# A new order of loads, stores and pieces in a cross-covariance attention kernel with a mixture of adapters

## The chip, the cores and the metric

The kernel runs on 1 core of one Trainium2 chip. The metric is device time in microseconds (us), the median of three runs.

## The reference

There are four batches, and in each of them q, k and v are 6400 x 256 in fp32. An attention over channels comes first, then a layer that adds two of eight small adapters to each row.

```python
qn = q / (np.linalg.norm(q, axis=1, keepdims=True) + 1e-06)
kn = k / (np.linalg.norm(k, axis=1, keepdims=True) + 1e-06)
s = kn.transpose(0, 2, 1) @ qn / tau          # 256 x 256 for each batch
a = np.exp(s - s.max(-1, keepdims=True)); a /= a.sum(-1, keepdims=True) + 1e-09
x = (v @ a).reshape(25600, 256)
logits = x @ w_gate                           # 8 experts, the best 2 are kept
w = softmax(logits of these two)
out = x + sum over the two experts of w * (x @ A[e]) @ B[e]      # A[e] is 256 x 16
```

Every input is read once and the output is written once: 78.91 MB read and 26.21 MB written by the profile's account.

## The kernel before, in words

**Tiling.** A batch of 6400 rows lies on 128 partitions as 50 columns of 256 numbers. One column of one input is 128 KB in HBM. q and k come in two loads of 25 columns each (`QK`, L248), some of them cut further (`PARTS`, L464). v comes in pieces of 10 columns, five for each batch, and `V` (L249) says which loads bring one piece and which bring two. The loads of q, k and v are issued by GpSimd (POOL, L690) and turn fp32 into bf16 on the way; only the first five columns of q and k come without it, from two other queues (L687). The stores are issued by SyncE (SP, L1033).

**What is done with the data.** For each column `do_G` (L699) adds k^T q to an accumulator in PSUM (L705), and on request k^T k and q^T q, whose diagonals are the squared norms (L709, L713). For a group of five columns named in `OFF` (L467) the squares are made elsewhere: ScalarE squares (L726) and VectorE adds (L732). When the 50 columns of a batch are in, a short chain (norms, L771, exp, L818, transposes, `waA`, `a`) makes the matrix a and the products of a with the gate and with A. From then on each piece of v can be worked on: ten transposes (`T`, L890) and their copies (`Te`), then logits and adapter inputs. Where the piece is in `MERGED` (L475) one matmul over 136 columns gives both (`ZL`, L914) and four copies bring them to SBUF; otherwise 8 columns of logits come first (`log`, L928, one copy) and the 128 of the adapter inputs later (`Z`, L981), read straight from PSUM. Eight small VectorE and ScalarE steps make the gate weights, `Ze` (L992) multiplies, `gzT` (L1004) transposes, `Y` (L1017 and L1022) makes the output in five parts, `Ye` (L872 or L874) copies them into a y slot, and the store leaves from there.

**What sets the order.** Nothing is scheduled by hand, line by line. `make_plan` (L281) lists every step with a duration, dependencies and a rank; `Plan.run` (L108) goes through them with a model of the engines, the clock and the DMA, and the order that comes out is what is emitted for each engine. The constants before the kernel's function steer this:

- `WORDS` (L454): the order of the loads. `q10` stands for the loads of q and k of batch 1, half 0, and `v32` for the load number 2 of v of batch 3.
- `STORE` (L255): buffers. There are 4 slots for halves of q and k, 4 slots for pieces of v, 4 for transposed pieces (`vT`) and 7 for pieces of the output (`y`). A load waits for its slots, and two pieces in one load need two neighbouring slots. At most 8 loads are outstanding (L79).
- `PAIRS` (L251): pieces whose output goes out in one store of 20 columns. `FINE` (L465): pieces of the last batch that go out in several stores.
- `HOLD` (L460): a store with an entry waits for the landing of the load that the entry names. This keeps the DMA engines for loads first and keeps stores in hand for later. The y slots stay taken as long. An entry for the second piece of a pair has no effect.
- `AHEAD` (L458) moves `T` and `ZL` forward in rank; `SQ` (L473) moves the squares; `WARM` (L457) allows for matmuls that only keep TensorE's clock up.

Of the kernel before, what the change touches and what calls it, by code (L numbers as in the profile page):

```python
# [71 lines left out]
class Plan:  # L72
# [35 lines left out]
    def run(self, head):  # L108
# [137 lines left out]
UNITS = ((0, 4), (4, 4), (8, 2))  # L246
GATE = {"eq1": "ga", "t": "ga", "th": "ga", "g2": "ga", "lm": "gb", "mask": "gb"}
QK = ((0, 25), (25, 25))  # L248
V = (((0, 1), (1, 1), (2, 2), (4, 1)), ((0, 1), (1, 1), (2, 1), (3, 2)), ((0, 1), (1, 1), (2, 1), (3, 1),  # L249
        (4, 1)), ((0, 1), (1, 1), (2, 2), (4, 1)))  # L250
PAIRS = {(0, 1), (1, 0), (2, 0), (2, 3)}  # L251

GROUPS = ((0, 5), (5, 5), (10, 5), (15, 5), (20, 5), (25, 5), (30, 5), (35, 5), (40, 5), (45, 5))
ZUNITS = ((0, 3), (3, 3), (6, 2), (8, 2))
# [3 lines left out]
def group_of(c):  # L258
    return max(g for g, (c0, _) in enumerate(GROUPS) if c0 <= c)
# [6 lines left out]
def load_of(b, i):  # L266
    return max(g for g, (i0, _) in enumerate(V[b]) if i0 <= i)


def pieces(b, i):  # L270

    return next((((b, j), (b, j + 1)) for j in (i - 1, i) if (b, j) in PAIRS), ((b, i),))


def held_by(p, b, i):

    kind, d, j = HOLD[b, i]
    return [k for k in p.steps if k[:4] == ("load", kind, d, load_of(d, j) if kind == "v" else j)][-1]


def make_plan(B, order, ahead):  # L281
# [6 lines left out]
    for kind, b, i in order:  # L288
        if kind == "v":
            c0, n = V[b][i]  # L290
            p.add(("load", "v", b, i, c0 * PC, n * PC), {}, (), 0, take=(("v", tuple((b, c0 + j) for j in range(n))),),
                  size=COL * n * PC)
            continue
        for c, n in PARTS.get((b, i), QK[i:i + 1]):
            for h in "qk":
# [3 lines left out]
    for h in "qk":  # L299
        p.add(("cast", h), {"ACT": 1.2}, [("load", h, 0, 0) + PARTS[0, 0][0]], 0)  # L300
    for b in range(B):

        for i, (c0, n) in enumerate(QK):
            for c in range(c0, c0 + n):
                deps = [k for k in p.steps if k[0] == "load" and k[2:4] == (b, i) and k[1] != "v"
                        and k[4] <= c < k[4] + k[5]]
                if (b, c) < (0, PARTS[0, 0][0][1]):
                    deps = [("cast", k[1]) for k in deps]
                if c:
                    deps.append(("G", b, c - 1))  # L310
                elif b:
                    deps += [(x, b - 1, ic) for x in ("n2", "accs") for ic in range(2)]
                p.add(("G", b, c), {"PE": 0.445 - 0.1135 * sum((b, group_of(c), w) in OFF for w in "kq")}, deps,
                      pos["qk", b, i] if b else -50,
# [3 lines left out]
        for w in "kq":  # L318
            halves = [x for x in range(len(GROUPS)) if (b, x, w) in OFF]
            if halves:  # L320
# [3 lines left out]
            for x, g in enumerate(halves):  # L324
# [3 lines left out]
                      [k for k in p.steps if k[:4] == ("load", w, b, i) and k[4] < c + n and c < k[4] + k[5]]  # L328
                      + [("cast", w)] * ((b, c) == (0, 0)), pos["qk", b, i] - SQ, take=(("ssq", ((w, b),)) if x == 0 else ("sq", ((w, b, g),)),),
                      give=(("qk", (w, b, i)),))  # L330
                if x:
                    p.add(("add", w, b, g), {"DVE": 0.069 + 0.2668 * n},
                          [("sq", w, b, g), before], pos["qk", b, i] - SQ, give=(("sq", (w, b, g)),))
                    before = ("add", w, b, g)
# [6 lines left out]
        if b == 0:  # L341
            p.add(("wts",), {"DVE": 2.12}, [("load", "k", 0, len(QK) - 1) + PARTS[0, len(QK) - 1][1]], -200)

# [21 lines left out]
        for i in range(NP):  # L365
            v = load_of(b, i)
            c0, n0 = V[b][v]
            x = pos["v", b, v] + 0.3 * (i - c0)
            for u, (c, n) in enumerate(UNITS):
# [4 lines left out]
                      [("T", b, i, u)], x - ahead, give=(("bank", ("T", b, i, u)),))  # L374
            merged = (b, i) in MERGED
            if merged:
# [54 lines left out]
    for b in range(B):  # L431
        for i in range(NP):
            x = pos["v", b, load_of(b, i)]
            names = pieces(b, i)
            if (b, i) != names[0]:
                continue
            parts = FINE[i] if b == B - 1 and i in FINE else ((0, PC * len(names)),)
            for c, n in parts:
                p.add(("store", b, i, c, n), {"SP": 0.46},
                      [("Ye", b, i + c0 // PC, c0 % PC) for c0 in range(c, c + n, 2)]  # L440
                      + ([held_by(p, b, i)] if (b, i) in HOLD else []), x, size=COL * n,
                      give=tuple(("y", x) for x in names) if c + n == PC * len(names) else ())
# [3 lines left out]
def make_order(words):  # L446

    order = [("qk", 0, i) for i in range(len(QK))]
    for w in words.split():
# [1 line left out]
    return order  # L451


WORDS = ('q10 v00 q11 v01 v02 q20 v03 v10 q21 v11 v12 v13 q30 v20 v21 v22 v23 q31 v24 v30 v31 v32 v33')  # L454
HEAD = 5.05
COL = 1.024 * 1.17647 / 32
WARM = 150  # L457
AHEAD = 5.7  # L458

HOLD = {(0, 0): ('v', 3, 2), (0, 1): ('v', 1, 4), (0, 2): ('v', 1, 2), (0, 3): ('k', 3, 1), (1, 0): ('v', 2,  # L460
        4), (1, 1): ('k', 3, 2), (1, 2): ('k', 3, 1), (1, 3): ('v', 3, 1), (2, 0): ('v', 3, 3), (2, 1):
        ('k', 2, 0), (2, 2): ('v', 1, 3), (2, 3): ('v', 2, 2), (3, 3): ('v', 2, 2)}

PARTS = {(0, 0): ((0, 5), (5, 12), (17, 8)), (0, 1): ((25, 17), (42, 8)), (3, 1): ((25, 17), (42, 8))}  # L464
FINE = {3: ((0, 6), (6, 4)), 4: ((0, 4), (4, 4), (8, 2))}  # L465
SPLIT, SHARES = set(), ()
OFF = {(0, 0, 'k'), (0, 0, 'q'), (0, 1, 'k'), (0, 2, 'k'), (0, 2, 'q'), (0, 3, 'k'), (0, 4, 'k'), (0, 4,  # L467
        'q'), (0, 5, 'q'), (0, 6, 'k'), (0, 7, 'k'), (0, 9, 'q'), (1, 0, 'k'), (1, 2, 'k'), (1, 3, 'k'), (1,
        3, 'q'), (1, 6, 'k'), (1, 6, 'q'), (1, 7, 'q'), (1, 8, 'k'), (1, 9, 'k'), (2, 0, 'k'), (2, 1, 'k'),
        (2, 3, 'k'), (2, 3, 'q'), (2, 4, 'k'), (2, 5, 'k'), (2, 5, 'q'), (2, 6, 'k'), (2, 6, 'q'), (2, 7,  # L470
        'q'), (2, 8, 'q'), (2, 9, 'q'), (3, 0, 'k'), (3, 1, 'k'), (3, 2, 'k'), (3, 2, 'q'), (3, 3, 'q'), (3,
        5, 'k'), (3, 5, 'q'), (3, 7, 'q'), (3, 8, 'q'), (3, 9, 'q')}
SQ = 0  # L473
SAFE = 1.3
MERGED = {(0, 0), (0, 1), (0, 2), (0, 3), (0, 4), (1, 0), (1, 1), (1, 2), (1, 3), (1, 4), (2, 0), (2, 2),  # L475
        (2, 3), (2, 4), (3, 0), (3, 1), (3, 2), (3, 3), (3, 4)}


def first_ahead(nc, names):
# [90 lines left out]
def kernel(  # L570
# [72 lines left out]
    scrap = const.tile([1, 16], BF16, name="scrap")  # L643
    order = make_order(WORDS)
    plan = make_plan(B, order, AHEAD)
    steps = plan.run(HEAD)
# [52 lines left out]
    def do_G(s, b, c):  # L699
# [4 lines left out]
        for ic in range(CC):  # L704
            nc.tensor.matmul(  # L705
                acc[ic][:, 0:256], kt[:, j, ic::CC], qt[:, j, :],
                start=c == 0, stop=False, skip_group_check=True)
            if (b, group_of(c), "k") not in OFF:
                nc.tensor.matmul(  # L709
                    acc[ic][:, 256:384], kt[:, j, ic::CC], kt[:, j, ic::CC],  # L710
                    start=False, stop=False, skip_group_check=True)
        for ic in range(0 if (b, group_of(c), "q") in OFF else CC):
            nc.tensor.matmul(  # L713
# [42 lines left out]
    def do_n2(s, b, ic):  # L756
# [5 lines left out]
        for x, w in enumerate("kq"):  # L762
            if all((b, g, w) in OFF for g in range(len(GROUPS))):
                continue
# [6 lines left out]
    def do_rsqrt(s, b):  # L771
        n2 = st[b]["n2"]
        for x, w in enumerate("kq"):
            part = held.get(("bank", ("n2p", w, b)))
            if part is None:
                continue
            if all((b, g, w) in OFF for g in range(len(GROUPS))):
                nc.vector.tensor_copy(n2[:, x, :], part)
# [97 lines left out]
    def do_cast(s, what):  # L876
        nc.scalar.copy(held["qk", (what, 0, 0), ""][:, 0:PARTS[0, 0][0][1], :], W[what])  # L877

# [58 lines left out]
    def gate_step(name):  # L937
        def f(s, b, i):
            if (b, i) in MERGED and name == "m1":
                gate_tiles(s, b, i)  # L940
# [87 lines left out]
    def do_store(s, b, i, c, n):  # L1028
# [3 lines left out]
        for rows in SHARES if (b, i) in SPLIT else (P,):  # L1032
            r = nc.sync.dma_start(out_v[b, p:p + rows, lo:lo + n, :], Y[p:p + rows, at_y:at_y + n, :])  # L1033
            if (b, i) in HOLD and not p:
                tc.add_manual_dep(r.ins, loaded[held_by(plan, b, i)],
# [62 lines left out]
```

## Time and profile before

| | |
|---|---|
| runs | 251.01, 251.12, 251.16 us, median 251.12 |
| profiled execution: span, first to last instruction | 246.2 us |
| last packet of a store in the profiled execution, from the first instruction on | 249.6 us |
| last store issued, and its landing | 244.8 us, 5.1 us later |
| TensorE, VectorE, ScalarE busy | 218.3, 184.8, 169.7 us |
| packet time on the 16 DMA engines, all queues | 102.3% of the span |

The time of the profiled execution as a whole isn't given apart from its span; the runs are 4.9 us longer than the span, and stores still move in 3.4 us of that. A share over 100% for the DMA engines means that records of neighbouring packets on an engine overlap in time. A load takes eight packets on each of the 16 engines (one for each partition row) and one of 4 bytes that reports its landing; a store likewise.

### The profile page before, as it was taken

How to read it: one execution, taken by the hardware profiler on the slowest of the kernel's cores; microseconds unless marked ns; L12 is line 12 of the kernel's file. 1: busy time of each engine (PE TensorE's matmuls, PEld its weight loads, DVE VectorE, ACT ScalarE, POOL GpSimd, SP SyncE). 2: the span in 40 equal slices, each digit the busy share in tenths (PEclk: the TensorE clock that was granted, in tenths of full speed). 3: DMA queues.
4: the chain of work that ended last, by engine and by line, in shares of the span. 5: the costliest groups of instructions: out<-in, count | busy, mean ns of one | idle time of the engine just before them, and what ended most of it. 6: DMA issues, size and time to landing. Idle time of an engine off the chain costs nothing.

```text
span 246.2 us, 5334 instructions
## 1 busy us (share of the span) xinstructions
PE 218.3 (89%) x2208; PEld 179.7 (73%) x2025; DVE 184.8 (75%) x511; ACT 169.7 (69%) x316; POOL 21.8 (9%) x45
## 2 busy tenths in 40 slices
PE   0687298498999999999969999999999999999996
PEld 0255175176877998978959788899776799999985
DVE  0045578558869689999974898998989578788681
ACT  2944442275666769888776787999453599988885
POOL 7000202100030011000201003110000000000000
PEclk9999769679999999999997999999999999999999
DMA  8999999999999999999999999999999999999999
GB/s 275 215 216 216 208 221 227 201 225 219 206 220 224 209 210 231 208 224 201 260 281 268 316 276 207 216 217 223 308 216 303 380 373 282 323 407 433 419 429 409
DMA packets 8788, 65.85 MB, mean 268 GB/s; under 512 B 994, under 2 KB 1378, under 8 KB 4796
## 3 DMA queue, kind: packets, MB, share of 16 engines
q0 software_dynamic: 5616, 38.67, 75.4%
q1 hardware_dynamic: 2812, 26.06, 25.6%
q10 hardware_dynamic: 336, 0.79, 0.8%
q8 instruction: 16, 0.26, 0.4%
q14 instruction: 8, 0.07, 0.1%
HBM read 78.91 MB, written 26.21 MB: 427 GB/s over the span
## 4 chain that ended last, share of the span: by engine, by line
DMA 39%; PE 37%; issue 11%; DVE 9%; ACT 3%; POOL 1%; POOLq 0%; ACTq 0%
DMA v<-in_v_dram 27%; PE Y_ps L1017 10%; DMA qk<-in_q_dram 6%; PE acc L705 6%; PE Y_ps L1022 5%; PE ZL_ps L914 5%; DMA qk<-in_k_dram 5%; PE T_ps L890 5%; PE gzT_ps L1004 3%; DVE gz L992 3%; DVE ssq L732 2%; PE acc L709 2%; ACT y L872 1%; DVE y L874 1%; PE acc L713 1%
## 5 line engine op out<-in xcount | busy, mean ns | idle before, releaser
L705 PE MATMUL acc<-qk 128*128 128x256 bf16 x400 | 77.6, 288 | 15.3 <-ACT qk L877 8.3
L732 DVE TENSOR_TENSOR ssq<-ssq,sq 128x1280 f32<-128x1280 f32 x35 | 52.0, 1487 | 21.9 <-ACT sq L726 21.9
L705 PEld LDWEIGHTS <-qk 128*128 128x128 bf16 x400 | 39.7, 104 | 31.0 <-DMA qk<-in_k_dram 9.8
L872 ACT COPY y<-Y_ps 128x512 f32<-128x512 f32 x87 | 50.8, 594 | 15.2 <-PE Y_ps L1022 12.9
L726 ACT ACTIVATE sq<-qk 128x1280 f32<-128x1280 bf16 x35 | 44.8, 1279 | 23.5 <-DVE ssq L732 20.7
L1017 PE MATMUL Y_ps<-a_bf,vT 128*128 128x256 bf16 x400 | 60.0, 272 | 0.1
L1017 PEld LDWEIGHTS <-vT 128*128 128x128 bf16 x400 | 38.3, 98 | 5.1 <-issue 0.4
L1022 PE MATMUL Y_ps<-ball,gzT 128*128 128x256 bf16 x200 | 38.2, 273 | 0.0
L992 DVE TENSOR_TENSOR gz<-zl,gatega 128x256 bf16<-128x256 f32 x95 | 35.4, 444 | 0.5
L709 PE MATMUL acc<-qk 128*128 128x128 bf16 x170 | 32.7, 225 | 0.0
L890 PE MATMUL T_ps<-ident,v 128*128 128x128 f32 x200 | 27.2, 284 | 3.9 <-DMA v<-in_v_dram 3.6
L713 PE MATMUL acc<-qk 128*128 128x128 bf16 x200 | 28.7, 227 | 0.0
L872 ACT COPY vT<-T_ps 128x512 f32<-128x512 f32 (+1 forms) x47 | 23.0, 545 | 5.5 <-PE T_ps L890 5.4
L890 PEld LDWEIGHTS T_ps<-ident,v 128*128 128x128 f32 x200 | 22.9, 146 | 5.3 <-issue 3.3
L914 PE MATMUL ZL_ps<-waA_sb,vT 128*128 128x136 bf16 x380 | 26.3, 223 | 0.4 <-ACT y L872 0.3
L914 PEld LDWEIGHTS <-vT 128*128 128x128 bf16 x380 | 23.8, 98 | 1.4 <-issue 0.4
L713 PEld LDWEIGHTS <-qk 128*128 128x128 bf16 x200 | 19.1, 102 | 5.0
L872 ACT COPY zl<-ZL_ps 128x408 f32<-128x408 f32 (+1 forms) x50 | 19.9, 457 | 3.4 <-PE ZL_ps L914 3.4
L1004 PE MATMUL gzT_ps<-ident,gz 128*128 128x128 f32 x100 | 19.8, 281 | 1.8 <-DVE gz L992 1.5
L1022 PEld LDWEIGHTS <-gzT 128*128 128x128 bf16 x200 | 19.5, 98 | 2.3
L874 DVE COPY zl<-ZL_ps 128x272 f32<-128x272 f32 (+1 forms) x26 | 12.7, 498 | 6.8 <-PE ZL_ps L914 6.6
L690 POOL DMA_DIRECT2D qk<-in_q_dram x11 | 6.1, 552 | 111.8 <-ACT y L872 41.2
(78 smaller groups left out, 217.2 us busy)
## 6 DMA issues: line engine op xcount, KB each, us to landing
out_dram<-y SPq DMA_DIRECT2D x10, 1280.0 KB, 11.8
out_dram<-y SPq DMA_DIRECT2D x4, 2560.0 KB, 17.5
v<-in_v_dram POOLq DMA_DIRECT2D x14, 640.0 KB, 28.0
qk<-in_q_dram POOLq DMA_DIRECT2D x5, 1600.0 KB, 15.9
qk<-in_k_dram POOLq DMA_DIRECT2D x5, 1600.0 KB, 23.0
v<-in_v_dram POOLq DMA_DIRECT2D x3, 1280.0 KB, 28.5
qk<-in_q_dram POOLq DMA_DIRECT2D x2, 1088.0 KB, 19.5
qk<-in_k_dram POOLq DMA_DIRECT2D x2, 1088.0 KB, 25.0
```

The lines of the kernel that those rows point to most:

```text
L705: nc.tensor.matmul(acc[ic][:, 0:256], kt[:, j, ic::CC], qt[:, j, :], start=c == 0, stop=False, skip_group_check=True)
L709: nc.tensor.matmul(acc[ic][:, 256:384], kt[:, j, ic::CC], kt[:, j, ic::CC], start=False, stop=False, skip_group_check=True)
L713: nc.tensor.matmul(acc[ic][:, 384:512], qt[:, j, ic * P:(ic + 1) * P], qt[:, j, ic * P:(ic + 1) * P], start=False, stop=c == NC - 1, skip_ ...
L726: nc.scalar.activation(out[:, 0:n, :], t[:, j:j + n, :], ACT.Square)
L732: nc.vector.tensor_tensor(out=t, in0=t, in1=held["sq", (w, b, g), ""][:, 0:n, :], op=OP.add)
L872: nc.scalar.copy(out, in_)
L890: nc.tensor.matmul(ps[:, j, :], vt[:, c + j, :].bitcast(FP32), W["ident32"], is_transpose=True, start=(j == 0), stop=(j == n - 1))
L914: nc.tensor.matmul(ps[:, j, :], vT_of(b, i, c + j)[:, :, ic], st[b]["waA"][:, ic, :], start=(j == 0 and ic == 0), stop=(j == n - 1 and ic ...
L992: nc.vector.tensor_tensor(out=pairs[:, h].rearrange("p c (e r) -> p c e r", e=E), in0=z[:, 2 * h:2 * h + 2, :].rearrange("p c (e r) -> p c ...
L1004: nc.tensor.matmul(ps[:, j, :], pairs[:, j * P:(j + 1) * P], W["ident32"], is_transpose=True, start=(j == 0), stop=(j == n // 2 - 1))
L1017: nc.tensor.matmul(ps[:, j, :], vT_of(b, i, c + j)[:, :, ic], st[b]["a"][:, ic, :], start=(j == 0 and ic == 0), stop=False, skip_group_che ...
L1022: nc.tensor.matmul(ps[:, j, :], pair[:, :, j], W["B"], start=False, stop=(j == 1), skip_group_check=True)
```

## The change

Only constants change. The order of the loads is new, v comes in seven loads of 20 columns and six of 10 (before: three and fourteen), q and k of the first half come in 5 + 20 columns (before 5 + 12 + 8), the first half of batch 1 in 17 + 8 (before 25). Five pairs of pieces share a store (before four), and of the last batch one piece goes out in two stores (before one in two and one in three), so 16 stores stand against 19. `HOLD`, `AHEAD` and `SQ` have new values, 48 groups of squares are off TensorE (before 43), and 10 pieces are merged (before 19).

```diff
-V = (((0, 1), (1, 1), (2, 2), (4, 1)), ((0, 1), (1, 1), (2, 1), (3, 2)), ((0, 1), (1, 1), (2, 1), (3, 1),
-        (4, 1)), ((0, 1), (1, 1), (2, 2), (4, 1)))
-PAIRS = {(0, 1), (1, 0), (2, 0), (2, 3)}
+V = (((0, 1), (1, 2), (3, 2)), ((0, 2), (2, 2), (4, 1)), ((0, 2), (2, 1), (3, 2)), ((0, 1), (1, 2), (3,
+        1), (4, 1)))
+PAIRS = {(0, 1), (1, 0), (1, 2), (2, 2), (3, 0)}
...
-WORDS = ('q10 v00 q11 v01 v02 q20 v03 v10 q21 v11 v12 v13 q30 v20 v21 v22 v23 q31 v24 v30 v31 v32 v33')
+WORDS = ('v00 q10 q11 v01 q20 v02 v10 q21 v11 v12 q30 v20 v21 q31 v22 v30 v31 v32 v33')
...
-AHEAD = 5.7
-
-HOLD = {(0, 0): ('v', 3, 2), (0, 1): ('v', 1, 4), (0, 2): ('v', 1, 2), (0, 3): ('k', 3, 1), (1, 0): ('v', 2,
-        4), (1, 1): ('k', 3, 2), (1, 2): ('k', 3, 1), (1, 3): ('v', 3, 1), (2, 0): ('v', 3, 3), (2, 1):
-        ('k', 2, 0), (2, 2): ('v', 1, 3), (2, 3): ('v', 2, 2), (3, 3): ('v', 2, 2)}
-
-PARTS = {(0, 0): ((0, 5), (5, 12), (17, 8)), (0, 1): ((25, 17), (42, 8)), (3, 1): ((25, 17), (42, 8))}
-FINE = {3: ((0, 6), (6, 4)), 4: ((0, 4), (4, 4), (8, 2))}
+AHEAD = 4.1
+
+HOLD = {(0, 0): ('v', 2, 4), (0, 2): ('v', 3, 4), (0, 3): ('v', 2, 4), (0, 4): ('k', 3, 0), (1, 0):
+        ('v', 3, 4), (1, 2): ('v', 3, 3), (1, 3): ('k', 1, 1), (1, 4): ('k', 1, 0), (2, 0): ('v', 3, 0),
+        (2, 1): ('v', 2, 3), (2, 3): ('v', 2, 1), (2, 4): ('k', 2, 1), (3, 0): ('v', 3, 0), (3, 2):
+        ('v', 3, 1), (3, 4): ('v', 3, 1)}
+
+PARTS = {(0, 0): ((0, 5), (5, 20)), (0, 1): ((25, 17), (42, 8)), (1, 0): ((0, 17), (17, 8)), (3, 1):
+        ((25, 17), (42, 8))}
+FINE = {4: ((0, 6), (6, 4))}
...
-SQ = 0
+SQ = -5.5
 SAFE = 1.3
-MERGED = {(0, 0), (0, 1), (0, 2), (0, 3), (0, 4), (1, 0), (1, 1), (1, 2), (1, 3), (1, 4), (2, 0), (2, 2),
-        (2, 3), (2, 4), (3, 0), (3, 1), (3, 2), (3, 3), (3, 4)}
+MERGED = {(0, 1), (0, 4), (1, 0), (1, 2), (2, 0), (2, 2), (2, 3), (3, 0), (3, 1), (3, 3)}
```

`OFF` has these groups for each batch (k and q; groups 0 to 4 are the first half):

| batch | before k | before q | after k | after q |
|---|---|---|---|---|
| 0 | 0 1 2 3 4 6 7 | 0 2 4 5 9 | 3 4 6 9 | 0 2 3 5 8 |
| 1 | 0 2 3 6 8 9 | 3 6 7 | 1 3 4 6 7 | 0 2 4 6 9 |
| 2 | 0 1 3 4 5 6 | 3 5 6 7 8 9 | 0 2 3 4 5 6 7 8 | 0 1 2 5 7 8 9 |
| 3 | 0 1 2 5 | 2 3 5 7 8 9 | 0 1 3 4 7 8 9 | 0 2 3 4 6 7 8 |

## The prediction, made before the changed kernel was run

> **What bounds the kernel now.** I read the page's 40 slices first, then its DMA queues and DMA issues, then the end of the chain of waits, and last the timeline of POOL, which issues the loads.
>
> ```profile
> PE   0687298498999999999969999999999999999996
> ...
> PEclk9999769679999999999997999999999999999999
> DMA  8999999999999999999999999999999999999999
> ```
>
> The row to look at is DMA: after the first slice the 16 engines are never under nine tenths, through every stage of the program. PE is full only from about 84 us on (155.55 of 162.3 us by the windows); the low clock at 24 to 48 us costs nothing that the DMA row shows.
>
> ```profile
> q0 software_dynamic: 5616, 38.67, 75.4%
> q1 hardware_dynamic: 2812, 26.06, 25.6%
> ...
> HBM read 78.91 MB, written 26.21 MB: 427 GB/s over the span
> ```
>
> Loads (q0, their bytes counted as bf16) and stores (q1) together fill the engines. The bytes are those of the reference and the change leaves them as they are.
>
> ```profile
> 244.00:245.00 1.00, 0.16 (x2) 0.00 (x0) 0.00 (x0) 0.71 (x2) 0.00 (x0) 1.00 1.02 422
> 245.00:246.30 1.30, 0.00 (x0) 0.00 (x0) 0.00 (x0) 0.00 (x0) 0.00 (x0) 1.00 1.00 407
> ```
>
> In these windows (length, then PE, PEld, DVE, ACT, POOL, clock, DMA share, GB/s) computing is over at 244.8 us and the DMA is still full.
>
> ```profile
> 243.94 0.23 PE Y_ps L1022 x2
> ...
> 244.19 0.59 ACT y L872
> ```
>
> That is the end of the chain of waits. The last store is issued at 244.8 us. By the packet records five of the 16 engines run dry at 247.2 us, eleven go on to 249.4 or 249.6, with stores issued earlier. So the end is that of the DMA work, and computing has a small slack. The kernel is at its floor: only shorter DMA work makes it faster, and a hole in the DMA or late computing makes it slower.
>
> **The sum's base.** The span is 246.2 us, the median 251.12; I keep the 4.9 us between them.
>
> **Part 1: fewer transfers.** The packet records, grouped by size, give the mean time of one packet. Loads: 399.5 ns for 10 columns, 474.1 for 12, 323.8 for 8, 662.2 for 17, 775.4 for 20, 964.6 for 25. Stores: 84.4 ns for 2 columns, 159.6 for 4, 234.9 for 6, 392.7 for 10, 767.1 for 20. The 4-byte record after a load takes 20.0 ns, after a store 12.6. Each transfer has eight packets and one such record on every engine.
> - Two v loads of 10 columns become one of 20, four times: 8 x (2 x 399.5 - 775.4) + 20 = 209 ns each, 0.83 us.
> - q and k of the first half join 12 + 8 into 20 (8 x 22.5 + 20 = 200 ns for each of the two), and batch 1 cuts 25 into 17 + 8 (8 x 21.4 + 20 = 191 ns for each): together nothing.
> - One more pair of pieces in a store: 8 x (2 x 392.7 - 767.1) + 12.6 = 159 ns. Piece 3 of the last batch whole instead of 6 + 4: 27 ns. Its piece 4 in 6 + 4 instead of 4 + 4 + 2: 85 ns. Together 0.27 us.
>
> That is 1.10 us of packet time on every engine, the upper end. The lower end is nothing, since neighbouring packets overlap. How much? All queues have 102.3% of 246.2 us, 251.9 us per engine, but the engines ran from about 1.0 to a mean of 248.6 us, 247.6 us: 4.3 us lie under other packets. The parts of the packets that don't grow with size are, from a line through the loads' means (22.2 ns a packet beside 37.7 a column), 8 x 22.2 + 20 = 198 ns for each of 39 loads, 7.7 us, and from the stores' (7.7 ns a packet) 74 ns for each of 19, 1.4 us. If the overlap hides these fixed parts, 4.3 of 9.1 us are hidden and 53% are paid. I take that share: 1.10 x 0.53 = **0.58 us**. Both ends, 0 and 1.10, stay for the range. Issuing seven transfers less (0.54 us each on POOL, 0.33 on SP) is worth nothing, both stand idle most of the time.
>
> A rule of the Trainium skill bears on this. DMA: Bandwidth & Descriptors, section Anatomy of one DMA, fits about 2.0 us of fixed cost for each DMA, so seven less would be 14 us; the section Rules for kernel authors says that this fixed cost overlaps when DMAs are issued early, by which the gain would be nothing. The rows here stand with the second, nearly: the engines have the next packets at hand, and what a transfer costs them is the tenths of a microsecond above.
>
> **Part 2: PE, ACT and DVE.** Nine pieces more are not merged. In the chain of waits ZL takes 1.18 us for a piece, log 0.48, and four Z matmuls 0.22, so Z 1.10: +0.40 us of PE each, +3.6 us. Five more groups of squares leave PE; at full clock the two matmuls of a column take 0.11 us in the timeline, 0.55 for a group: -2.8 us. PE gets +0.8 us in all, but in batches 2 and 3, where it is full, seven groups leave and three more pieces are unmerged: -3.9 + 1.2 = -2.7 us. The +3.5 us of batches 0 and 1 fall mostly ahead of or around 84 to 130 us.
>
> ```profile
> L732 DVE TENSOR_TENSOR ssq<-ssq,sq 128x1280 f32<-128x1280 f32 x35 | 52.0, 1487 | 21.9 <-ACT sq L726 21.9
> ...
> L726 ACT ACTIVATE sq<-qk 128x1280 f32<-128x1280 bf16 x35 | 44.8, 1279 | 23.5 <-DVE ssq L732 20.7
> ```
>
> Five squares add 5 x 1.279 = 6.4 us of ACT and 5 x 1.487 = 7.4 us of DVE (third number after the bar: mean ns). Nine unmerged pieces drop two copies of 507 and two of 398 ns each and add one of 231: -14.2 us. In sum nothing. DVE works 134.6 and ACT 125.6 of 162.3 us from 84 us on, which takes the shift. Price on the end: nothing, while the DMA has work.
>
> **Part 3: order, holds, slots.** Does the DMA always have work? Issued but not yet moved loads and stores, from issue times and packet sizes, are worth least in these places: 6.6 us at 26.7, 6.9 at 69.2, 6.3 at 91.1, 5.1 at 206.1, 2.4 at 246.
>
> ```profile
> 26.78 0.54 POOL L690 DMA_DIRECT2D qk<-in_q_dram  x1 [20.43 <-ACT sq L726]
> ...
> 69.28 0.54 POOL L690 DMA_DIRECT2D qk<-in_q_dram  x1 [25.42 <-ACT y L872]
> ```
>
> The first places are POOL's waits for slots of q and k, all loads behind them queue on POOL too. At 0.30 us a column: `v00` moves ahead of `q10` and adds 3.0 us of cover at 26.7 us. The 20-column load of k lands at about 18.7 us, when the 8 columns do now, instead of 13.8 for the 12; `G` of 20 columns takes about 6.6 us at full clock and 13 at half, so `q10` is asked for by 32 us at the latest, and the cover lasts beyond 36. Ahead of `q20` stand 230 columns instead of 240, which takes 3.0 us off the 6.9; but the 17-column cut brings the first of batch 1 six columns, 1.9 us, sooner than now. Price: nothing, cover about 4 us there.
>
> Late in the program the holds shift. Now six of the seven y slots are held until 182 to 185 us (k half 1 and v piece 4 are waited for), then four come free. After the change pieces 0 to 3 of batch 1, four slots, are held until the last two loads land, about 205 us (600 columns of loads, some 80 of stores). Three slots serve the rest meanwhile. At the very end the last store has 4 columns instead of 2, 8 x 160 = 1.28 us instead of 0.67; behind the other stores' backlog it costs nothing unless it is issued after 246.0 us: the floor's end 249.0 less the 2.4 us from the issue to the first dry engine now, less 0.6. That is 1.2 us later than the 244.8 of now.
>
> **Sum.** -0.58 + 0 + 0 = 251.12 - 0.58 = **250.5 us**.
>
> **The rivals.**
> - **A, all of the packet time is paid**: 251.12 - 1.10 = 250.0 us. For it: the DMA row has no holes. Against: the overlap of 2.3%.
> - **B, all of it is hidden**: 251.1 us, no change. For it: fixed parts of nine packets are small beside 3 to 8 us of data. Against: the means of 10 and 20 columns differ by clearly less than twice.
> - **C, slower: y slots run short between 182 and 205 us.** A store takes 11.8 us from issue to landing (median of 10 columns), 17.5 for a pair; a piece takes PE 1.1 + 1.18 + 0.55 + 3.28 = 6.1 us. Three slots over 6.1 + 11.8 us make a piece each 6.0 us, just PE's pace; with pairs, 6.1 + 17.5 over 3 is 7.9, and PE idles 1.8 us a piece, 7 us in four pieces, of which early T and ZL of two pieces (4.6) fill some. 2.6 us remain, 1.2 are slack: 250.5 + 1.4 = 251.9 us, up to 253 if nothing fills. It decides from 1.2 us of lateness on. For it: the output of piece 1 of batch 2 is stretched over 12 us now (187 to 200). Against: PE stays busy there all the same.
> - **D, a hole in the loads**: `q20` or a 20-column v load, which needs two neighbouring slots, is asked for late by more than its cover. Each microsecond of hole costs one; one or two would give 251.5 to 252.5 us. For it: POOL's waits are for slots throughout. Against: cover of 4 us and more.
>
> **How the numbers follow.** 0.2% is 0.5 us, about what a measurement of this kernel can tell from no change, and the forecast stands just beyond it. Forecast 0.42 (of it 0.12 end within the bound), A 0.12, B 0.13, C 0.22, D 0.11. Faster 0.30 + 0.12 = 0.42, within 0.25, slower 0.33. The range goes from A, 249.9, to C's and D's middle, 252.4; the likeliest case alone has 250.2 to 250.8.
>
> **What would show it.** Right: the DMA row full from the second slice to the last, packet time of all queues near 250.8 us per engine, the last y copy before 246 us with stores still moving after it. C shows as idle PE between 180 and 210 us with y copies waiting for stores, and a last copy after 246; D as a slice under 9 in the DMA row behind a late POOL issue; A and B as a saving of 1.1 or 0 with the DMA full. What would make it wrong above all is a schedule that lets the DMA engines stand.

## The result and the profile after

The changed kernel is **slower**: median 254.97 us (254.31 to 255.62 in four runs) against 251.14 us (251.01 to 251.19) for the kernel before on the same chip. The ratio is 1.0136, with a 95% interval of 1.0113 to 1.0158. In three of the later runs (1, 9 and 10) one execution took 258.5 to 258.6 us, over 1.5% more than the fastest of its kernel, and the ratios leave it out. Its lines stand two further down in the code than those of before (loads L692, copies L874 and L876, `T` L892, `ZL` L916, `Z` L983, `Y` L1019 and L1024, stores L1035).

| profiled execution | before | changed |
|---|---|---|
| span, us | 246.2 | 246.9 |
| last y copy ends | 244.8 | 245.5 |
| first of the 16 DMA engines out of work | 247.0 | 249.9 |
| last store lands | 249.9 | 253.5 |
| whole execution | runs: median 251.12 | 255.62 |

The last copy is 0.7 us later, the landing 3.6 us. So the transfers are late, far more than the computing is. The page of the changed kernel hides it:

```profile
PE   0649498589888999799999999999989999999996
...
PEclk9997979979999999999999999999999999999999
DMA  8999999999999999999999999999999999999999
GB/s 278 219 214 217 208 222 214 208 231 212 215 219 214 218 218 212 305 297 257 214 208 226 218 212 253 285 210 235 301 211 364 388 263 207 273 422 424 414 440 420
...
q0 software_dynamic: 5040, 38.67, 75.5%
q1 hardware_dynamic: 2394, 25.39, 24.8%
...
HBM read 78.91 MB, written 26.21 MB: 426 GB/s over the span
```

The DMA row is as full as before: a slice is 6.2 us long, and a gap of half a microsecond doesn't show in its tenths. The GB/s row gives a hint at its 33rd figure (263, at 198 to 204 us), but a load counts there with its bf16 bytes and a store with its fp32 bytes, so that row also falls when loads take the place of stores. The 34th figure, 207, is such a fall: from 202 to 210 us the changed kernel moves as much data as the other.

What settles it is the count of columns moved. I added up the packet records of loads and stores, a column being 128 rows of one input or of the output; a full DMA moves 13.1 of them in 4 us, whichever kind.

```
columns moved up to ... us     182     186     190     198     202     210     214     230     246
before                       581.0   593.9   606.8   632.6   645.7   671.5   684.5   736.4   788.1
changed                      581.6   593.9   606.3   630.7   641.1   667.2   676.4   728.2   780.2
changed minus before          +0.5    +0.0    -0.5    -1.9    -4.6    -4.4    -8.1    -8.2    -7.9
```

Up to 182 us the changed kernel is a little ahead (0.5 column, 0.16 us). From there to 214 us it loses 8.6 columns, 8.6 / 13.1 x 4 = 2.6 us, and keeps the deficit to the end. Narrow windows (length; PE, PEld, DVE, ACT, POOL busy; clock, DMA share, GB/s), first of the changed kernel and then of before, show two different losses:

```profile
182.00:186.00 4.00, 4.00 (x43) 3.37 (x38) 3.96 (x10) 2.06 (x6) 0.00 (x0) 1.00 0.93 192
...
194.00:198.00 4.00, 3.98 (x44) 3.76 (x42) 3.60 (x7) 4.00 (x11) 1.07 (x2) 1.00 0.89 371
198.00:202.00 4.00, 4.00 (x56) 3.67 (x53) 2.94 (x14) 2.95 (x8) 0.53 (x1) 1.00 1.03 265
...
210.00:212.00 2.00, 2.00 (x29) 1.95 (x27) 2.00 (x7) 1.72 (x6) 0.00 (x0) 1.00 1.09 161
```

```profile
194.00:198.00 4.00, 3.80 (x33) 3.28 (x33) 2.80 (x16) 3.96 (x9) 0.53 (x1) 1.00 1.08 437
198.00:202.00 4.00, 4.00 (x41) 3.63 (x40) 3.49 (x11) 3.65 (x9) 0.00 (x0) 1.00 1.01 374
...
210.00:212.00 2.00, 2.00 (x28) 1.88 (x26) 1.60 (x5) 1.57 (x4) 0.00 (x0) 1.00 0.94 323
```

At 182 to 186 and 194 to 198 us the share falls to 0.93 and 0.89: **engines stand dry**, 0.75 us between 184 and 198 us by the gaps in the packet records. At 198 to 202 and 210 to 212 us the share is over 1, yet little is moved (161 GB/s at 210 to 212 us, where loads alone made 211 at 204 to 208): the **packets themselves are slow**. Their mean times in these stretches:

```
                        before            changed
198.5 to 203 us   loads of 20    774 ns       884 ns (61 packets)
                  stores of 10   398 ns       452 ns (38)
210.4 to 213.6    loads of 10    398 ns       635 ns (79)
```

Why do engines run dry at 184 us? The timeline of POOL in the changed kernel, loads of v only (start, length, what is issued and how often, idle time before and what ended it), and then that of before:

```profile
159.38 1.07 POOL L692 DMA_DIRECT2D v<-in_v_dram  x2 [4.93 <-PE T_ps L892]
196.81 1.07 POOL L692 DMA_DIRECT2D v<-in_v_dram  x2 [36.36 <-PE gzT_ps L1006]
198.12 0.53 POOL L692 DMA_DIRECT2D v<-in_v_dram  x1 [0.24 <-issue]
```

```profile
162.72 0.53 POOL L690 DMA_DIRECT2D v<-in_v_dram  x1 [2.68 <-PE gzT_ps L1004]
165.59 0.53 POOL L690 DMA_DIRECT2D v<-in_v_dram  x1 [2.34 <-PE T_ps L890]
196.37 0.53 POOL L690 DMA_DIRECT2D v<-in_v_dram  x1 [30.25 <-PE T_ps L890]
```

Before, piece 1 of batch 3 is a load of its own, asked for at 165.59 us, as soon as one v slot is free. In the changed kernel it comes with piece 2 in one load. One slot is free there just as early (the `T` of piece 2 of batch 2 ends at 164.7 us), but the joined load waits for two neighbouring slots, which come free with the `T` of pieces 3 and 4 of batch 2, the later at 196.5 us. (The issue follows that `T` by 0.3 us; the view names a `gzT` of the same engine.) POOL idles for 36.36 us and then asks for three loads at once. Ten columns that were in hand before are missing at 184 to 198 us, and the stores at hand don't fill their place.

The end of the chain of waits of the changed kernel, against the `y` copy at 244.19 us of before:

```profile
240.48 0.67 PE Z_ps L983 x12
244.93 0.59 ACT y L874
```

The landing's delay is then 2.6 us of lost DMA work and 0.6 us from the last store, which has 4 columns instead of 2 (1.28 against 0.67 us by the prediction's packet means); 0.4 us remain of the 3.6. The sum is rough: by the packet records 15 of the 16 engines are done at 251.8 us, and the last 1.2 us before the landing are the eight packets of the last store on one engine that was behind. Another 0.9 us lie between the landing and the end of the execution (255.62 - 253.47 = 2.15 us, against 251.12 - 249.88 = 1.24, with the median of before for its profiled execution; the changed kernel's profiled execution was the slowest of its four). The packet records show a 16 KB instruction fetch at 254.8 us there, and none after 233 us in before. In the profile of run 1, the same kernel, one stands at 254.5 us and the stretch is 2.23 us; in the eleven other runs none comes after the last landing, and it is 1.34 to 1.62 us. So the 0.9 us go with that fetch, though no run was made to take it away.

### The profile page after: what moved, and what is told of

Same layout as the page of the kernel before. It is cut to its first block, busy times and chain, and to the rows that moved or that the text cites. A ratio compares the mean times of both kernels' runs of the same rounds, so it can differ in the third digit from the quotient of the medians.

```text
span 246.9 us, 5564 instructions
## 1 busy us (share of the span) xinstructions
PE 217.6 (88%) x2336; PEld 178.8 (72%) x2166; DVE 186.9 (76%) x510; ACT 164.7 (67%) x300; POOL 19.3 (8%) x41
## 4 chain that ended last, share of the span: by engine, by line
PE 48%; DMA 35%; DVE 9%; ACT 5%; issue 2%; POOL 1%; POOLq 0%; ACTq 0%
DMA v<-in_v_dram 22%; PE Y_ps L1019 13%; DMA qk<-in_q_dram 7%; PE acc L707 7%; DMA qk<-in_k_dram 7%; PE Y_ps L1024 7%; PE T_ps L892 6%; PE gzT_ps L1006 4%; DVE ssq L734 4%; PE Z_ps L983 3%; PE ZL_ps L916 3%; ACT sq L728 2%; DVE gz L994 1%; PE acc L715 1%; PE acc L711 1%
## 5 line engine op out<-in xcount | busy, mean ns | idle before, releaser
L734 DVE TENSOR_TENSOR ssq<-ssq,sq 128x1280 f32<-128x1280 f32 x40 | 59.4, 1485 | 30.1 <-ACT sq L728 29.8
L728 ACT ACTIVATE sq<-qk 128x1280 f32<-128x1280 bf16 x40 | 51.1, 1279 | 29.2 <-DVE ssq L734 13.8
L1019 PE MATMUL Y_ps<-a_bf,vT 128*128 128x256 bf16 x400 | 60.0, 272 | 0.0
L874 ACT COPY y<-Y_ps 128x512 f32<-128x512 f32 x76 | 43.6, 591 | 10.3 <-PE Y_ps L1024 8.5
L1019 PEld LDWEIGHTS <-vT 128*128 128x128 bf16 x400 | 38.6, 98 | 4.4
L1024 PE MATMUL Y_ps<-ball,gzT 128*128 128x256 bf16 x200 | 38.2, 273 | 0.0
L892 PE MATMUL T_ps<-ident,v 128*128 128x128 f32 x200 | 26.4, 275 | 4.2 <-DMA v<-in_v_dram 3.6
L874 ACT COPY vT<-T_ps 128x512 f32<-128x512 f32 (+1 forms) x43 | 21.4, 558 | 9.8 <-PE T_ps L892 9.7
L892 PEld LDWEIGHTS T_ps<-ident,v 128*128 128x128 f32 x200 | 21.7, 141 | 6.1 <-ACT waA_sb L860 1.9
L874 ACT COPY gzT<-gzT_ps 128x256 f32<-128x256 f32 (+1 forms) x47 | 15.5, 342 | 10.7 <-PE gzT_ps L1006 10.6
L1024 PEld LDWEIGHTS <-gzT 128*128 128x128 bf16 x200 | 19.5, 98 | 2.5 <-DVE gzT L876 0.2
L994 DVE TENSOR_TENSOR gz<-Z_ps,gatega 128x256 bf16<-128x256 f32 x50 | 19.1, 439 | 2.4 <-PE Z_ps L983 2.0
L994 DVE TENSOR_TENSOR gz<-zl,gatega 128x256 bf16<-128x256 f32 x50 | 19.3, 443 | 0.1
L876 DVE COPY y<-Y_ps 128x512 f32<-128x512 f32 x24 | 16.1, 686 | 1.7 <-PE Y_ps L1024 1.6
L1006 PEld LDWEIGHTS gzT_ps<-ident,gz 128*128 128x128 f32 x100 | 12.4, 140 | 6.2 <-DVE gz L994 2.3
L983 PE MATMUL Z_ps<-waA_sb,vT 128*128 128x128 bf16 x200 | 14.9, 219 | 0.6 <-DVE gz L994 0.6
```

What stands on the lines that cost most here:

```text
L728: nc.scalar.activation(out[:, 0:n, :], t[:, j:j + n, :], ACT.Square)
L734: nc.vector.tensor_tensor(out=t, in0=t, in1=held["sq", (w, b, g), ""][:, 0:n, :], op=OP.add)
L874: nc.scalar.copy(out, in_)
L892: nc.tensor.matmul(ps[:, j, :], vt[:, c + j, :].bitcast(FP32), W["ident32"], is_transpose=True, start=(j == 0), stop=(j == n - 1))
L983: nc.tensor.matmul(ps[:, j, :], vT_of(b, i, c + j)[:, :, ic], st[b]["aA"][:, ic, :], start=(j == 0 and ic == 0), stop=(j == n - 1 and ic = ...
L994: nc.vector.tensor_tensor(out=pairs[:, h].rearrange("p c (e r) -> p c e r", e=E), in0=z[:, 2 * h:2 * h + 2, :].rearrange("p c (e r) -> p c ...
```

## The experiments

**The theory** (T1): the joined load of pieces 1 and 2 of batch 3 is asked for 31 us later than the single load could be; the hole of 184 to 198 us and the slow packets behind it come of that. **The rivals**: (R1) the hole is one of work of any kind, so that a store let go earlier would fill it; (R2) larger transfers don't save what was thought, or cost something themselves; (R3) the pieces that are no longer merged make computing late, and the end follows computing. Each run has its own median of before on the same chip beside it (251.4 to 252.1 us).

**1. The changed kernel once more** (`after_again`, no edit).

> The changed kernel once more, as the control of this call. Theory 1 (the DMA engines run dry): 254 to 256 us, and the profile again shows a DMA share under 0.95 somewhere between 184 and 202 us, where three v loads wait for two neighbouring slots until about 197 us. Rival (loads of the late stage move slowly by themselves, the waiting loads are a side show): the same time, but the slow packets stand somewhere else than right behind the dry stretch.

Measured: ratio 1.0158 [1.0114, 1.0203]. The deficit against before is 4.2 columns at 202 us and 7.7 at 214, with slow packets at 198 to 203 and 210 to 213 us again. The places belong to the kernel, not to one execution.

**2. The joined load cut in two** (`after_v31_split`): piece 1 goes into the slot that is free at 164 us and is asked for there; pieces 2 and 3 move to the slots 0 and 1. In the code `n` is the place of the joined load and `free` that of the last `T` of piece 2 of batch 2.

```diff
+    at["v", (3, 1)], at["v", (3, 2)], at["v", (3, 3)] = 3, 0, 1
...
+    first.key, second.key = ("load", "v", 3, 1, 10, 10), ("load", "v", 3, 1, 20, 10)
+    steps[n] = second
...
+    steps.insert(free + 1, first)
...
```

> The changed kernel, but pieces 1 and 2 of v of batch 3 come in two loads of 10 columns instead of one of 20: the first goes into the slot that has been free since about 164 us and is asked for then, the second into the slot freed at about 191 us. Nothing else in the order changes. Theory 1 (dry engines behind a load that needs two neighbouring slots): no window under 0.97 of DMA share after 184 us, and the time falls by all that was lost there, 2.6 us of DMA work by the cumulated columns, to 251 to 252.5 us. Rival A (only the hole itself, 0.75 us, comes from the waiting loads; the slow packets of 199 to 203 and 210 to 214 us are their own matter): 254 to 254.5 us. Rival B (computing is late, since TensorE has more to do): no change.

Measured: 1.0047 [1.0028, 1.0065]. About two thirds of the loss is gone. The timeline of POOL in this kernel:

```profile
164.79 0.53 POOL L701 DMA_DIRECT2D v<-in_v_dram  x1 [4.52 <-PE T_ps L901]
191.96 0.53 POOL L701 DMA_DIRECT2D v<-in_v_dram  x1 [26.64 <-PE T_ps L901]
```

Its windows at the two old places, and at a new one:

```profile
198.00:202.00 4.00, 4.00 (x55) 3.65 (x53) 3.92 (x17) 3.33 (x9) 0.61 (x2) 1.00 1.03 319
210.00:212.00 2.00, 2.00 (x28) 1.88 (x26) 1.31 (x4) 1.79 (x4) 0.00 (x0) 1.00 0.99 302
...
230.00:234.00 4.00, 4.00 (x39) 3.61 (x37) 3.73 (x20) 3.52 (x9) 0.00 (x0) 1.00 0.73 303
234.00:238.00 4.00, 4.00 (x45) 3.70 (x43) 2.06 (x6) 3.21 (x8) 0.00 (x0) 1.00 0.77 328
```

The dry stretch and the slow packets of 184 to 214 us are gone together (loads of 10 take 398 ns at 198.5 to 203 us, stores of 10 400 ns). But at 230 to 238 us the DMA is dry with PE busy 4.00 of 4.00 us in both windows: now the DMA waits for computing, and 6.2 columns (1.9 us) are lost there. By this reading the changed kernel had the second shortage too, and its own lateness covered it: it was 8 columns behind at 230 us, so that much was still in hand.

**3. A store let go earlier instead** (`after_pair_early`): the held store of pieces 2 and 3 of batch 1 goes out behind that of piece 3 of batch 0 (`n`), and is held by the same load as that one.

```diff
+    steps.insert(n + 1, pair)
...
-                tc.add_manual_dep(r.ins, loaded[held_by(plan, b, i)],
+                hold = (0, 3) if (b, i) == (1, 2) else (b, i)
+                tc.add_manual_dep(r.ins, loaded[held_by(plan, *hold)],
```

> The changed kernel, but the store of pieces 2 and 3 of batch 1, 20 columns, no longer waits for the last load but one: it waits for the load of pieces 3 and 4 of batch 2 like its two neighbours and is issued behind them at about 188 us. The loads are as slow to be asked for as before. Theory 1 (dry engines): 6 us more of DMA work are at hand in the dry stretch, the time falls to 251 to 252.5 us. Rival A: by 0.75 us at most, to 254. A rival on slots (it is the v slots that matter, and the stores only push the late loads back further): no gain or slower.

Measured: 1.0263 [1.0222, 1.0305]. The dry stretch of 184 to 198 us is filled, and the time is longer still. R1 falls: the store moves in front of the late loads. These land at 213.2, 219.4 and 225.9 us instead of 207.9, 211.0 and 218.7, computing follows, and later the DMA has nothing to move at all. Slow packets stand behind the filled stretch as well, at 199 to 206 us, so they don't need dry engines ahead of them. The later windows:

```profile
222.00:226.00 4.00, 4.00 (x55) 3.63 (x52) 3.57 (x18) 3.45 (x10) 0.00 (x0) 1.00 0.65 178
...
234.00:238.00 4.00, 4.00 (x61) 3.77 (x59) 3.05 (x17) 3.50 (x11) 0.00 (x0) 1.00 0.54 224
238.00:242.00 4.00, 4.00 (x41) 3.60 (x39) 2.33 (x8) 3.53 (x8) 0.00 (x0) 1.00 0.39 164
```

PE is full in all of them, so it is behind. What was missing at 184 us wasn't just any work for the DMA, but that load.

**4. What a transfer costs, in the kernel before** (`before_seven_more`): the three loads of v of 20 columns and the four pair stores each go out in two, from the same places of the order (`step` is 10 for a load of 20).

```diff
+        for x in range(0, n, step):
+            loaded[s.key] = nc.gpsimd.dma_start(t[:, x:x + step, :], src[b, :, c + x:c + x + step, :]).ins.name
...
+            if n > PC:
+                nc.sync.dma_start(out_v[b, p:p + rows, lo + PC:lo + n, :], Y[p:p + rows, at_y + PC:at_y + n, :])
```

> The kernel before with its three v loads of 20 columns and its four stores of pairs each cut into two of 10 columns, issued back to back: seven transfers more, the change's saving turned round, in a kernel whose DMA engines are never dry. The prediction's step: 1.26 us more by packet times (3 x 0.209 + 4 x 0.159), 0.67 us at the 53% that it took to be paid, so 251.8 us. If the overlap hides all of it: 251.1; if all of it is paid: 252.4.

Measured: 1.0023 [1.0003, 1.0042], +0.58 us with an interval of 0.08 to 1.05. By the prediction's packet prices these seven would be worth 8 x (2 x 399.5 - 775.4) + 20 = 209 ns three times and 159 four times, 1.26 us, and at its share of 53% 0.67. The 0.58 us need not all be the price of transfers: by columns this kernel is 1.4 behind at 230 us (0.43 us), and at 238 to 246 us its engines stand dry for another 0.3 us, since the last store is issued 1.7 us later than in before. So the price that the prediction took is not contradicted, the full packet time lies outside the interval, and the first half of R2 falls: larger transfers do save something. Run 9 tests the other half.

**5. Load and first store both single** (`after_split_both`): as 2, and pieces 0 and 1 of batch 3, a pair in one store, go out one by one, the first right behind its copies (`done` is the last `Ye` of piece 0).

```diff
+    alone.key, other.key = ("store", 3, 0, 0, 10), ("store", 3, 1, 0, 10)
+    steps[n] = other
...
+    steps.insert(done + 1, alone)
...
```

> The changed kernel with pieces 1 and 2 of v of batch 3 loaded singly (as in the run before it) and, besides, pieces 0 and 1 of batch 3 stored singly as each is done. With the first edit alone the profile shows a second dry stretch at 230 to 238 us, 6.3 columns or 1.9 us, while the pair of stores waits for its second piece until 234.5 us. Theory 1, extended (the second loss is a store that isn't there, behind which computing has 1 to 2 us of lateness): piece 0 leaves at about 226 us, the dry stretch shrinks to 1 us or less, the time falls from 1.0047 of before to 0.999 to 1.002. Rival (computing as a whole sets the end now, the last store is issued at 247 us whatever the DMA does): no change from 1.0047.

Measured: 1.0055 [1.0036, 1.0075], no gain over 2. The first of the two stores goes out at 227.4 us, where the pair went at 234.2, and the gap only moves. In this kernel:

```profile
230.00:234.00 4.00, 4.00 (x39) 3.62 (x38) 3.70 (x20) 3.47 (x10) 0.00 (x0) 1.00 0.96 404
234.00:238.00 4.00, 4.00 (x45) 3.71 (x43) 2.06 (x6) 3.43 (x8) 0.00 (x0) 1.00 1.00 414
238.00:242.00 4.00, 4.00 (x41) 3.62 (x40) 0.46 (x2) 3.26 (x7) 0.00 (x0) 1.00 0.72 300
```

The last store is issued at 247.0 us, against 244.8 in before. The size of the pair isn't what sets the end; PE is full in all three windows, and run 11 tests whether its pace does.

**6. Cut, and both halves asked for late** (`after_split_late`): as 2, with both halves behind the last `T` of piece 4 of batch 2 (`free`) in program order.

```diff
+    steps[free + 1:free + 1] = [first, second]
```

> The changed kernel with the same two single loads, into the same slots, but both asked for as late as the load of 20 columns was, at about 197 us. If it is the early asking that helped (theory 1), this run is as slow as the changed kernel, 1.013 to 1.018 of before, with the dry stretch at 184 to 200 us and slow packets behind it. If it is the size of the load or the two neighbouring slots in themselves, it is as fast as the run with one early load, 1.005.

Measured: 1.0079 [1.0055, 1.0103]. It didn't test what it was built for: POOL issued the first half at 164.65 us all the same, and the second at 191.82, as in 2. Nothing stood ahead of the first on POOL's queue and its slot was free, and the place among other engines' instructions did not hold it back. So it is a second run of 2, with the dry stretch at 230 to 238 us again; the two intervals overlap.

**7. The single load of before moved behind** (`before_v31_late`): in before, the load of piece 1 of batch 3 (`late`) stands directly before that of pieces 2 and 3 (`n`), and the store that was held by it is held by an earlier load.

```diff
...
+    steps.insert(n, late)
+    HOLD[1, 3] = ("v", 3, 0)
```

> The kernel before with its single load of piece 1 of v of batch 3 asked for just ahead of the next one, at about 196 us instead of 165.6, and the store that waited for it (piece 3 of batch 1) held by the load before it instead. The ring of loads is empty from 191 to 198 us, but 60 columns of stores are at hand from 186 us on. Theory 1 (what counts is that the engines have any work): little or nothing lost, 1.000 to 1.003. Rival C (a ring of loads that runs empty and starts again makes slow packets, stores or not, as the run with the early pair of stores had them at 199 to 206 us): slow packets at 198 to 204 us and 1 to 2 us lost, 1.004 to 1.008.

Measured: 1.0001 [0.9986, 1.0016]. For the same reason as in 6 the load went out at 165.6 us. All it tells is that this hold doesn't matter: the store left at 191.1 instead of 197.6 us and nothing came of it.

**8. Three joins in before** (`before_joined`): the single loads of v of pieces 1 and 2 of batch 1, 0 and 1 of batch 2, and 2 and 3 of batch 2 become loads of 20, at the place of the later one.

```diff
+    for b, i, j in ((1, 1, 2), (2, 0, 1), (2, 2, 3)):
+        steps.remove(next(s for s in steps if s.key[:4] == ("load", "v", b, i)))
...
+        second.key = ("load", "v", b, j, i * PC, 2 * PC)
...
```

> The kernel before with six of its v loads of 10 columns joined into three of 20 where the slots are neighbours and the two were asked for within 2 us of each other: three transfers less without a new order. By packet times 0.63 us less, at the 53% taken in the prediction 0.33 us: 0.9987 of before; all hidden 1.0000; all paid 0.9975. If the later landing of piece 1 of batch 1, by 3 us, matters: slower by up to 0.3 us.

Measured: 0.9991 [0.9980, 1.0002], no difference. Three transfers less, but piece 1 of batch 1 lands at 120.0 us instead of 117.1, computing lags from there on, and the last store is issued at 247.3 instead of 244.8 us. The single loads of this piece and the next were asked for 0.5 us apart, so it isn't a late slot that costs here, but the landing of the first piece together with the second. A join gives and takes; here it came out even.

**9. Cut in two, and made to wait for the late slots** (`after_split_waiting`): both halves are single loads, but the first on POOL's queue is the one whose slot comes free at 196 us, so the other, whose slot is free, stands behind it.

```diff
+    at["v", (3, 1)], at["v", (3, 2)], at["v", (3, 3)] = 3, 1, 0
...
+    steps[free + 1:free + 1] = [second, first]
```

> The changed kernel with pieces 1 and 2 of v of batch 3 in two single loads, both made to wait on GpSimd's queue: piece 2 goes first, into the slot freed at about 196 us, and piece 1 stands behind it, so that both are asked for at about 197 us as the load of 20 columns is. Theory 1 (the early asking is what helped): as slow as the changed kernel, 1.012 to 1.018, dry at 184 to 200 us, slow packets behind. If the size of the load makes the loss: 1.005. (The earlier run that meant to ask late did not: GpSimd issued its first half at 165 us all the same, since its slot was free and nothing stood ahead of it.)

Measured: 1.0110 [1.0081, 1.0139]. This is the run that 6 should have been. Its timeline of POOL:

```profile
159.09 1.06 POOL L701 DMA_DIRECT2D v<-in_v_dram  x2 [4.82 <-PE T_ps L901]
196.52 2.23 POOL L701 DMA_DIRECT2D v<-in_v_dram  x4 [36.37 <-PE gzT_ps L1015]
```

and its windows:

```profile
182.00:186.00 4.00, 4.00 (x42) 3.37 (x38) 3.97 (x10) 1.76 (x5) 0.00 (x0) 1.00 0.90 186
...
198.00:202.00 4.00, 4.00 (x55) 3.71 (x53) 2.95 (x15) 2.65 (x7) 0.64 (x2) 1.00 0.97 240
```

The dry engines and the slow packets (at 198.5 to 203 and 210.4 to 213.6 us loads of 10 take 454 and 601 ns on average instead of 398) are back although no load of 20 is in that place. So the size of the transfer isn't it, and the rest of R2 falls; the late asking is.

**10. Less work for TensorE in the changed kernel** (`after_less_z`): the three pieces of the last two batches that the change no longer merges ((2,4), (3,2), (3,4)) make only half of their `Z`.

```diff
-            for ic in range(CC):
+            last = 1 if (b, i) in ((2, 4), (3, 2), (3, 4)) else CC
+            for ic in range(last):
```

> The changed kernel without half of the Z matmuls (the second half of the contraction) of the three unmerged pieces of the last 45 us, pieces 4 of batch 2 and 2 and 4 of batch 3: 30 matmuls, 1.65 us of TensorE, are left out, and the adapter inputs of these pieces with them. Theory 1 (in the changed kernel DMA sets the end, 6 us of stores are waiting when the last is issued): no change, 1.012 to 1.018. Rival (TensorE in the tail sets it): 1.6 us less, 1.006 to 1.010.

Measured: 1.0113 [1.0087, 1.0139], below the 1.0136 and 1.0158 of the changed kernel, with intervals that overlap, so a gain of some tenths of a per cent isn't excluded. The last store is issued 1.1 us earlier (244.4 instead of 245.5 us) and lands at nearly the same time (253.36 against 253.47). Its profiled execution is 0.9 us shorter than that of the changed kernel, and 0.8 of this lies behind the landing, where this one has no instruction fetch. In the changed kernel the DMA sets the end, and R3 explains at most a small part of its loss.

**11. The same in the mended kernel** (`after_split_both_less_z`): the edits of 5 and 10 together.

> The version with the two single loads and the two single stores, and the same half of Z of three pieces left out. Theory 2 (once the dry stretch is mended, TensorE is the bound of the last 40 us, where three unmerged pieces put 1.9 us more on it than the kernel before has): the last store is issued at about 245.7 us instead of 247.3, and the time falls by 1.2 to 1.6 us, from 1.0055 to 0.999 to 1.001. Rival (stores and their slots set the end): no change.

Measured: 1.0015 [0.9999, 1.0032], against 1.0055 [1.0036, 1.0075] without the second edit: 0.4%, 1.0 us, for 1.65 us of TensorE less, and the intervals don't overlap. Once the hole is mended R3 holds. The execution that was profiled was the slowest of this kernel's runs, with dry stretches at 210 to 212 and 238 to 242 us, so I read nothing finer from its trace.

**12. Two joins in before** (`before_joined_two`): as 8 without the one in batch 1.

```diff
+    for b, i, j in ((2, 0, 1), (2, 2, 3)):
...
```

> The kernel before with two joined pairs of v loads, pieces 0 and 1 and pieces 2 and 3 of batch 2, whose later landing meets work that starts later still (the join of pieces 1 and 2 of batch 1, which landed 3 us late for its first piece, is left out). Two transfers less: 0.42 us less by packet times, 0.22 at 53%: 0.9983 to 0.9996 of before, unless a late landing costs it again.

Measured: 0.9984 [0.9970, 0.9998], -0.40 us with an interval of -0.75 to -0.05. Its windows at the critical places and at the end:

```profile
198.00:202.00 4.00, 4.00 (x40) 3.62 (x40) 3.53 (x12) 3.69 (x8) 0.00 (x0) 1.00 1.02 374
210.00:212.00 2.00, 2.00 (x27) 1.87 (x25) 1.56 (x5) 1.81 (x5) 0.00 (x0) 1.00 0.97 325
...
230.00:234.00 4.00, 4.00 (x39) 3.64 (x37) 3.23 (x14) 3.42 (x9) 0.00 (x0) 1.00 0.97 409
```

The DMA stays as full as before and the last store is issued at 244.8 us as before. The gain has the size that two transfers less would give, but the profile doesn't show it: by columns this execution leads by 0.1 (0.03 us) from 182 us to the end, and its last store lands at 250.4 us, later than the 249.9 of before. It is the only version here whose interval lies below 1, and that by little.

## Why the prediction was wrong

**What bounds the kernel** was right: before, the DMA work sets the end, and 10 shows that it still does in the changed kernel. What is lost there stays lost: of the 8.1 columns missing at 214 us 7.9 are missing at 246.

**Part 1, fewer transfers, -0.58 us (0 to -1.10)**, is not contradicted in price. Seven transfers more cost 0.58 us [0.08, 1.05], some of it late computing, where that price gives 0.67; two fewer gave 0.40 [0.05, 0.75], not seen in the columns moved, where it gives 2 x 209 ns = 0.42 in full and 0.22 at 53%. In the changed kernel itself only the lead of 0.16 us at 182 us is seen of it. The intervals don't settle the share of 53%.

**Part 2, "Price on the end: nothing"**, held for the changed kernel, but for a reason that it didn't have. Its sum for batches 2 and 3, -3.9 us of squares and +1.2 us of unmerged pieces, mixes two stages. All squares are done by 207 us; the work of the unmerged pieces lies almost wholly behind 204 us. By the groups of TensorE after 204 us, the `ZL` of five pieces, 6.7 us in before,

```profile
L914 PE MATMUL ZL_ps<-waA_sb,vT 128*128 128x136 bf16 x100 | 6.7, 223 | 0.0
```

stand against these in the changed kernel:

```profile
L983 PE MATMUL Z_ps<-waA_sb,vT 128*128 128x128 bf16 x60 | 4.4, 219 | 0.0
L916 PE MATMUL ZL_ps<-waA_sb,vT 128*128 128x136 bf16 x60 | 4.0, 222 | 0.2 <-DVE waA_sb L862 0.2
L930 PE MATMUL log_ps<-waA_sb,vT 128*128 128x8 bf16 x40 | 1.3, 166 | 0.0
```

That is 9.7 against 6.7 us of busy time. Half of the difference is the `Z` of piece 4 of batch 2, whose `ZL` in before ran ahead of 204 us; the five pieces of batch 3 alone take 8.2 against 6.7, 1.5 us more for two unmerged pieces, where the prediction's 0.40 us a piece gives 0.8. (Busy times of neighbouring matmuls overlap, so these are upper figures.) The DMA's lateness covered it. Runs 2, 5 and 11 show what is behind the cover: with the hole mended, 0.5% to the bad (1.2 to 1.4 us), of which 1.0 us goes when half of those `Z` go.

**Part 3, "Does the DMA always have work?"**, is the step that failed: it put the new loads at a price of nothing, and they cost 2.6 us of DMA work. It checked the cover at the two waits for slots of q and k (26.7 and 69.2 us) and the y slots at 182 to 205 us, and found no price. At the first two nothing was lost: the changed kernel is ahead at 182 us. It never followed POOL's waits for v slots: the trace of before had the single load at 165.59 us and a wait of 30.25 us behind it, and the new `V` joins just that load to the one after the wait. The prediction's backlog numbers for before contained these ten columns, and the joined load takes them away at 184 us.

**Rival C, the y slots**, was not seen: the last copy is at 245.5 us, ahead of its mark of 246, and PE is busy for 10.79 and 11.74 of 12 us at 180 to 192 and 192 to 204 us (11.46 and 11.80 in before). **Rival D** named the mechanism with its condition ("a 20-column v load, which needs two neighbouring slots, is asked for late by more than its cover"), at a chance of 0.11 and a price of 1 to 2 us; the loss was 3.8 by the medians. Its rule "each microsecond of hole costs one" counted dry time alone. The dry time was 0.75 us up to 198 us and 0.2 more up to 202; most of the other 1.65 of the 2.6 us of lost DMA work are slow packets, which no row of before had shown in this stage. On top of the 2.6 come the larger last store (0.6 us, which the prediction had priced at nothing unless issued after 246 us) and, in the profiled execution, the 0.9 us behind the landing. Its test, a slice under 9 in the DMA row, was too coarse: no slice fell.

**What stays open.** Why packets are slow at 198 to 203 and 210 to 213 us. They came in all runs in which the late loads were asked for at 197 us (the changed kernel twice, 9, 10, and in 3 at 199 to 206 us) and in none in which the first of them was asked for at 165 us (2, 5, 6, 11), so in this kernel late asking brings them on; how it does so was not tried. Run 8 doesn't fit: 24 slow packets of its last load stand at 215 to 218 us, though its single load was asked for at 168.0 us. Open as well is why the instruction fetch comes behind the last landing in some executions and whether it costs the 0.9 us.

## What to carry to other kernels

Joining two transfers on a full DMA saved one or two tenths of a microsecond here at most, and it makes the pair wait for the later of two buffers and the first piece for the landing of both. Look up in the trace when the single one was issued before you join, and join only where both slots come free together (not so in the change) and the first piece isn't wanted before both have landed (not so in 8; run 12 has both). A row of busy shares in tenths doesn't show a loss of 1%: add up the bytes moved and lay two kernels side by side. Work that moves between stages counts only in the stage where its engine is full, so sum it there, and expect a shortage that one delay covers to appear when that delay is mended.

## What the runs showed of the hardware

- A DMA share over 1 can go with seven tenths of the rate: in the changed kernel it is 1.03 at 210 to 214 us, where 9.2 columns move instead of 13.0 (share 0.99 in before) and packets of 10 columns take 635 ns on average instead of 398. The share says that packets are in flight, not that bytes move.
- The slow packets are on all engines at once: the records of 210 to 213 us fall into 16 rows of adjoining packets, and each row has some. Packets of the same size run at full speed a little earlier (399 ns at 204 to 209 us). Apart from these stretches and the one of run 8, slow packets stand in numbers only at 1 to 4 us (5 columns of q, 293 ns on average in before and 278 in the changed kernel, against 199 and 204 ns for those of k).
- POOL issued a load as soon as its slot was free and nothing stood ahead of it on POOL, 31 to 32 us ahead of its place in the program's order among the other engines (6, 7). What did hold a load back was a waiting load ahead of it on POOL's own queue (9).
- A transfer of 10 or 20 columns cost 0.08 us of the program's time (seven more; 0.06 by the columns moved) to 0.20 us (two fewer, not seen in the columns), with intervals for one transfer of 0.01 to 0.15 and 0.03 to 0.38 us.
